# Word conversions five to each of the first three batches, the last one at the beginning of the fourth

## The chip, the cores and the metric

The kernel runs on one core of one Trainium2 chip. The metric is the device time of one execution in microseconds (us). Engines: PE is TensorE, DVE is VectorE, ACT is ScalarE, POOL is GpSimd, and SP is SyncE, which issues all the kernel's DMAs from one queue.

## The reference, cut to what matters

Three layers follow one another: attention over a small memory, a mixture of eight experts that picks one expert per token, and a gated feed-forward layer.

```python
def reference(**kwargs):
    ...
    attn_out = _attn_ref(**attn_kwargs)
    B, H, S, D = attn_out.shape                      # 4, 8, 576, 64
    x = np.ascontiguousarray(attn_out.transpose(0, 2, 1, 3)).reshape(B, S, H * D)
    x = _moe_ref(x=x, **moe_kwargs)
    return _moe2_ref(x=x, **moe2_kwargs)

def _moe2_ref(x, w_in, conv_w, w_out):
    B, S, D_ff = (*x.shape[:2], w_in.shape[1])       # 4, 576, 1024
    K = conv_w.shape[0]                              # 3
    h = np.maximum(x @ w_in, 0.0)
    ...                                              # conv_out: three taps of conv_w along the tokens
    gate = 1.0 / (1.0 + np.exp(-conv_out))
    return (h * gate @ w_out).astype(np.float32)
```

The two weights of the last layer, `w_in` (512 x 1024) and `w_out` (1024 x 512), arrive as 64-bit floats. The kernel reads them as pairs of 32-bit words and turns them into 32-bit floats on the chip. This is the "word conversion".

## The kernel before, in words

**Two phases.** In the first phase the four batches b = 0 to 3 go through attention and through the expert of the batch's first token. In the second phase (`gated`, L801) the four batches go through the last layer: per batch eight blocks f of hidden columns (`pi`, PSUM from `banks`, two buffers, L159), each followed on ACT and DVE by the chain `ht` (L839), `ct` (L841), the two convolution steps (L842, L844), the sigmoid (L820), the product (L821) and the split into `g` (L825, by the helper lines L170 on ACT and L171 on DVE or POOL). Then the output product `po` (L860) runs over all `g` of the batch.

**The written order.** `order()` (L62) writes out the order of the first phase. Each batch has 24 places i: places 0 to 7 are `h` (six matmuls each, `ph`), 8 to 11 are `y` (24 matmuls each, `py`), then again eight `h` and four `y`. After each place the list `after[i]` names further work. PE follows this list exactly (`manual_schedule`, L722). For the other engines and for the DMA queue the order is fixed when the kernel is built, by a planner that goes by the program's order, by what depends on what, and by an estimate of the times. It is not decided anew while the kernel runs: each engine works through its list in order.

**A word conversion.** There are 16, numbered 0 to 15: 0 to 7 make `w_in`, 8 to 15 make `w_out`. Number i has a load of 512 KB into a `words` tile (two buffers, L273, L274), then two ACT steps (L234 takes the size of the high words, L240 scales the low words) and seven DVE steps (L235 to L239, L241, L242), which use two tiles `nd` and `nt` of the tag `nar` (two buffers in all, L281, L282), and a store of 256 KB to `f_in` or `f_out` in DRAM (L284). So number i+1 can't write its `nt` before number i has read its own for the last time (L241), nor its `nd` before the store of i has landed. The load of i+2 can only start when i has read its words for the last time (L242). L234 is held behind what the program put on ACT before it (`keep_in_program_order`); nothing holds L240 back but its load. `narrow_next()` (L75) puts conversion i at a place and, behind it, the load of i+2. The first two loads stand after place 0 of batch 0.

**Who needs them.** `wi0` to `wi3` are loaded from `f_in`, `wo0` to `wo3` from `f_out`, `wo3` from conversions 14 and 15.

**Memory between the phases.** The tiles `vw`, `h`, `words`, `nar` and `ys` of the first phase lie in one pool (`ffn`, L621). It is closed at L892, and the pool of `g`, `tail` and `ot` opens behind it (L893) on memory that it left, each tile waiting for the tiles that it covers (`reuse_waits="tile"`). `ht` and `ct` share six buffers of the tag `cv` (L838, L840, pool at L696). A `ct` is held until its `g` has been split.

Of the kernel before, what the change touches and what calls it, by code (L numbers as in the profile page):

```python
# [57 lines left out]
def units(b):  # L58
    return 2 * b, 2 * b + 1


def order():  # L62

    held = [0]

    def each(c, *parts):
        return [f"{part}.{u}" for u in units(c) for part in parts] if c < B else []  # L70

    def of(c, *parts):
        return [f"{part}.{c}" for part in parts] if c < B else []

    def narrow_next():  # L75

        i = held.pop(0) if held else 16
        return ([f"nar.{i}"] if i < 16 else []) + [f"nload.{i + 2}"] * (i < 14) + (held.append(i + 1) or [])

    out = ["phi.0", "phi.1", "gates", "kv.0", "kv.1", "phi.2", "phi.3", "q.0", "q.1", "kv.2", "kv.3"]  # L80
    out += each(0, "psoft") + each(0, "pback") + each(1, "psoft") + ["mem.0", "mem.1", "back.0", "back.1", "gatew.0", "gatew.1", "frow.0"]
    out += ["fcol.0", "flog.0", "pback.2", "scores.0.0", "scores.1.0", "ssoft.0.0", "ssoft.1.0"]
    out += ["asplit.0.0", "asplit.1.0", "pback.3", "scores.0.1", "scores.1.1", "ssoft.0.1", "ssoft.1.1"]
    out += each(1, "mem") + each(1, "back") + ["asplit.0.1", "asplit.1.1", "vw.0.0", "q.2", "q.3", "gatew.2", "gatew.3", "vw.0.1"]
    for b in range(B):
        c, d = b + 1, b + 2
        u, v = units(c)
        whole = c < B
        after = {i: [] for i in range(24)}
        for i, more in {  # L90
            1: of(c, "frow"),
            3: [f"scores.{u}", f"ssoft.{u}"] * whole,
            8: of(c, "fcol") + [f"scores.{v}", f"ssoft.{v}"] * whole,
            9: of(c, "flog"),
            10: each(d, "pback"),
            11: each(d, "mem")[:1],
            12: each(c, "asplit"),
            13: each(d, "mem")[1:],
            16: each(d, "back"),
            18: each(d, "gatew"),  # L100
            19: of(c, "rtok"),
            21: of(c, "vw0"),
            22: of(c, "vw1"),
        }.items():
            after[i] += more

        if d < B:
            after[2] += each(d, "phi", "kv")
            after[8] += each(d, "psoft")
            after[14] += each(d, "q")  # L110
        if b == 0:
            after[0] += ["w2.0.0", "w2.0.1", "nload.0", "nload.1"]
            after[2] += ["w2.0.2", "w2.0.3"]
            after[9] += ["rtok.0"]
        else:
            after[1] += [f"w2.{b}.3"]
        if whole:
            for i, j in ((21, 0), (22, 1), (23, 2)):
                after[i] += [f"w2.{c}.{j}"]
            for i in (5, 9, 13, 17):  # L120
                after[i] += narrow_next()
            if b == 1:
                after[18] += ["conv"]
        else:
            after[0] += ["rall"]
            after[5] += ["rpp"]
            after[8] += ["rown"]
            after[9] += ["close"]
            for i in (10, 12, 14, 16):
                after[i] += narrow_next()  # L130
            for kc, i in enumerate((12, 14, 17, 20)):
                after[i] += [f"win.{kc}"]
        for i in range(24):
            out += [f"h.{b}" if i % 12 < 8 else f"y.{b}"] + after[i]
    return out
# [6 lines left out]
def fused_kernel(tc, q, first, kv, kv_tail, phi, w1, w2, w_in, conv_w, w_out, out):  # L142
# [3 lines left out]
    with (  # L146
# [565 lines left out]
        def stage_expert(b, g):  # L712
# [6 lines left out]
            "win": lambda kc: stage_w1(lambda: src_in, kc, f"wi{kc}"),  # L719
        }  # L720
        plan = order()
        with tc.manual_schedule(engines={ENG.PE}):  # L722
            for table in (loads, do):
# [228 lines left out]
```

## Time and profile before

| what | value |
|---|---|
| time, median of 3 runs | 456.09 us (455.87 to 458.81) |
| the profiled execution, its own time | 460.18 us |
| its span, first to last instruction | 458.4 us |
| PE busy / DVE busy / ACT busy / POOL busy | 429.5 / 304.2 / 226.1 / 42.2 us |
| mean granted TensorE clock | 0.987 of full speed |

The profiled execution took 1.8 us more than its span, and is 4.1 us longer than the median of the three runs. A busy time counts an engine from the start to the end of its instructions. The ends of matmuls are modelled, so the progress of PE is read better from the number of matmuls in a stretch than from its busy share. "Idle before" an instruction is the time for which its engine stood still, with what ended that.

### The profile page before, as it was taken

What the parts mean: (1) busy time and instruction counts of PE and PEld (TensorE: products, weight loads), DVE (VectorE), ACT (ScalarE), POOL (GpSimd) and SP (SyncE); (2) the same over time, 40 slices, a digit from 0 to 9 for tenths busy, and PEclk for the clock granted to TensorE, in tenths of its full rate; (3) what the DMA queues carried; (4) which work ended last, traced back from release to release, by engine and by line L of the source; (5) the groups of instructions that cost most, each with busy time, mean ns of one, the idle gap of its engine ahead of it and who ended that gap; (6) DMA issues with size and microseconds to landing.
All of it is one profiled execution on the core that took longest, in us unless ns stands there. A gap on an engine that the chain in (4) does not pass through costs nothing.

```text
span 458.4 us, 7910 instructions
## 1 busy us (share of the span) xinstructions
PE 429.5 (94%) x3082; PEld 382.5 (83%) x3083; DVE 304.2 (66%) x566; ACT 226.1 (49%) x432; POOL 42.2 (9%) x64
## 2 busy tenths in 40 slices
PE   3588999998999899999999959999999999999994
PEld 2345898887988689979999958899988998899884
DVE  2379974679956698796899789637920688058700
ACT  4347455454453534456736547247731675157511
POOL 1000000000000000000000006201420043003400
PEclk9999989899999999999999989999999999999999
DMA  7999979443695406988554311320002000100011
GB/s 250 345 346 375 352 284 371 134 159 126 198 358 156 154 15 193 388 292 297 130 190 153 129 49 43 104 92 1 1 35 79 3 2 0 70 23 1 1 71 51
DMA packets 28750, 69.02 MB, mean 151 GB/s; under 512 B 3200, under 2 KB 8576, under 8 KB 28704
## 3 DMA queue, kind: packets, MB, share of 16 engines
q1 hardware_dynamic: 28704, 68.43, 43.9%
q8 instruction: 26, 0.43, 0.4%
q14 instruction: 20, 0.16, 0.1%
HBM read 51.82 MB, written 16.59 MB: 149 GB/s over the span
## 4 chain that ended last, share of the span: by engine, by line
PE 82%; DVE 5%; DMA 5%; ACT 2%; issue 2%; SPq 1%; ACTq 0%
PE po L860 21%; PE py L181 21%; PE pi L181 19%; PE ph L181 10%; PE pv L632 3%; DMA kv<-in_kv 2%; PE pl L514 2%; PE pk L383 2%; PE sc L407 2%; DMA wo2r<-f_out 1%; DMA n4r<-in_w_in 1%; DMA n9r<-in_w_out 1%; DVE wb L171 1%; PE pa L369 1%; PE pfb L486 1%
## 5 line engine op out<-in xcount | busy, mean ns | idle before, releaser
L181 PEld LDWEIGHTS py<-h,wb 128*128 128x128 f32 x768 | 105.9, 194 | 6.3 <-issue 2.9
L181 PE MATMUL py<-h,wb 128*128 128x288 f32 x768 | 110.9, 302 | 0.0
L181 PE MATMUL pi<-yh,wi 128*128 128x288 f32 x512 | 92.1, 298 | 4.8 <-ACT ht L839 4.8
L860 PE MATMUL po<-wo,g 128*128 128x512 f32 (+1 forms) x408 | 89.8, 377 | 0.0
L860 PEld LDWEIGHTS po<-wo,g 128*128 128x128 f32 x408 | 73.0, 188 | 13.4
L181 PEld LDWEIGHTS pi<-yh,wi 128*128 128x128 f32 x512 | 77.3, 191 | 6.0 <-ACT ht L839 5.3
L842 DVE SCALAR_TENSOR_TENSOR ct<-ht,convw,ct 128x575 f32<-128x575 f32 x32 | 30.4, 950 | 51.6 <-ACT ct L841 51.6
L181 PE MATMUL ph<-att,vh 128*128 128x288 f32 x256 | 53.8, 303 | 3.4 <-DVE h L646 3.4
L826 POOL CAST tail<-g 128x128 fp32r<-128x128 f32 x32 | 22.4, 706 | 373.9 <-DVE g L171 373.3
L181 PE MATMUL pi<-yl,wi 128*128 128x288 f32 x256 | 55.2, 297 | 0.0
L181 PEld LDWEIGHTS ph<-att,vh 128*128 128x128 f32 x256 | 40.5, 188 | 7.6 <-DVE h L646 5.2
L181 PEld LDWEIGHTS pi<-yl,wi 128*128 128x128 f32 x256 | 41.6, 191 | 0.0
L839 ACT ACTIVATE ht<-pi 128x576 f32<-128x576 f32 x32 | 20.8, 651 | 36.6 <-PE pi L181 35.7
L645 ACT ACTIVATE h<-ph 128x288 fp32r<-128x288 f32 x64 | 25.4, 410 | 25.6 <-PE ph L181 25.5
L181 PE MATMUL ph<-att,vl 128*128 128x288 f32 x128 | 37.6, 294 | 0.0
L646 DVE SCALAR_TENSOR_TENSOR h<-ph,h 128x288 fp32r<-128x288 f32 x64 | 27.4, 444 | 10.4 <-ACT h L645 10.4
L821 DVE TENSOR_TENSOR ct<-ht,ct 128x576 f32<-128x576 f32 x32 | 27.9, 871 | 6.7 <-ACT ct L820 6.5
L884 ACT ACTIVATE ot<-po 128x512 f32<-128x512 f32 x17 | 9.5, 598 | 41.6 <-PE po L860 41.6
L690 ACT ACTIVATE ys<-py 128x288 f32<-128x288 f32 x32 | 13.0, 407 | 31.7 <-PE py L181 16.6
L170 ACT ACTIVATE g<-ct 128x576 fp32r<-128x576 f32 x32 | 21.3, 679 | 13.8 <-DVE ct L821 13.8
L844 DVE SCALAR_TENSOR_TENSOR ct<-ht,convw,ct 128x575 f32<-128x575 f32 x32 | 26.0, 811 | 0.2
L841 ACT ACTIVATE ct<-ht,convw 128x576 f32<-128x576 f32 x32 | 24.6, 769 | 1.3 <-DVE ct L821 1.0
(246 smaller groups left out, 546.2 us busy)
## 6 DMA issues: line engine op xcount, KB each, us to landing
kv<-in_kv SPq DMA_DIRECT2D x8, 1024.0 KB, 12.2
q<-in_q SPq DMA_DIRECT2D x8, 576.0 KB, 8.7
ydram<-ys SPq DMA_DIRECT2D x32, 144.0 KB, 2.3
y<-ydram SPq DMA_DIRECT2D x4, 1152.0 KB, 5.6
out<-ot SPq DMA_DIRECT2D x15, 256.0 KB, 2.2
ph<-in_phi SPq DMA_DIRECT2D x8, 288.0 KB, 9.9
adram<-at SPq DMA_DIRECT2D x8, 288.0 KB, 6.4
wa_0r<-in_w SPq DMA_DIRECT2D x4, 512.0 KB, 4.1
```

Source lines behind the costliest of these rows:

```text
L170: nc.scalar.activation(hi, src, AF.Copy)
L181: nc.tensor.matmul(ps, st, mv[:, cols], start=i == 0, stop=i == len(terms) - 1)
L632: nc.tensor.matmul(ps[slot_rows(pr)], vs[:, slot_rows(pr)], raws[pr][:, cols], start=True, stop=True)
L645: nc.scalar.activation(t[:, 0, :], ps, AF.Relu)
L646: nc.vector.scalar_tensor_tensor(t[:, 1, :], ps, 0.0, t[:, 0, :].bitcast(F32), ALU.max, ALU.subtract)
L821: slow(f"gm.{f}").tensor_tensor(ct, ht, ct, ALU.mult)
L826: nc.gpsimd.tensor_copy(tail[:, f, :, to:to + 64], t[:, :, 512:576].bitcast(F32))
L839: nc.scalar.activation(two(ht), halves(ps), AF.Relu)
L841: nc.scalar.activation(ct, ht, AF.Copy, scale=convw[:, 1, f:f + 1])
L842: nc.vector.scalar_tensor_tensor(ct[:, 1:], ht[:, :S - 1], convw[:, 0, f:f + 1], ct[:, 1:], ALU.mult, ALU.add)
L844: nc.vector.scalar_tensor_tensor(ct[:, :S - 1], ht[:, 1:], convw[:, 2, f:f + 1], ct[:, :S - 1], ALU.mult, ALU.add)
L860: nc.tensor.matmul(ps[:, cols], st[sp], w[:, mp, f % 2, cols], start=f == 0 and i == 0, stop=f == 7 and i == 2)
```

## The change

Conversions stand after other places. In batches 0 to 2 there are five each, after places 4, 7, 10, 13 and 16, where there were four after places 5, 9, 13 and 17. So these batches hold conversions 0 to 14 instead of 0 to 11. In batch 3, number 15 stands after place 1, where numbers 12 to 15 stood after places 10, 12, 14 and 16. The call after place 3 of batch 3 comes to number 16, which doesn't exist, and adds nothing. Each conversion takes its store and the load of the next but one along. No instruction is added or removed.

```diff
         if whole:
             for i, j in ((21, 0), (22, 1), (23, 2)):
                 after[i] += [f"w2.{c}.{j}"]
-            for i in (5, 9, 13, 17):
+            for i in (4, 7, 10, 13, 16):
                 after[i] += narrow_next()
             if b == 1:
                 after[18] += ["conv"]
         else:
...
             after[5] += ["rpp"]
             after[8] += ["rown"]
             after[9] += ["close"]
-            for i in (10, 12, 14, 16):
+            for i in (1, 3):
                 after[i] += narrow_next()
             for kc, i in enumerate((12, 14, 17, 20)):
                 after[i] += [f"win.{kc}"]
```

## Rows read from the trace of the kernel before

**Rows 1.** The page, part 1: busy time, share of the span, instructions.

```profile
PE 429.5 (94%) x3082; PEld 382.5 (83%) x3083; DVE 304.2 (66%) x566; ACT 226.1 (49%) x432; POOL 42.2 (9%) x64
```

**Rows 2.** Stretches: length, busy us (count) of PE, PEld, DVE, ACT, POOL; clock; DMA; GB/s.

```profile
42.00:99.90 57.90, 57.19 (x473) 50.62 (x471) 44.09 (x91) 29.98 (x66) 0.00 (x0) 0.94 0.80 274
99.90:155.50 55.60, 54.14 (x463) 47.10 (x462) 43.56 (x93) 27.16 (x61) 0.00 (x0) 1.00 0.60 203
155.50:205.00 49.50, 48.15 (x356) 42.73 (x356) 40.51 (x92) 22.83 (x47) 0.00 (x0) 1.00 0.58 202
252.60:277.60 25.00, 20.21 (x142) 19.74 (x141) 19.53 (x30) 14.63 (x23) 3.13 (x4) 0.93 0.31 101
277.60:300.00 22.40, 22.40 (x103) 18.63 (x102) 16.56 (x20) 10.47 (x18) 7.68 (x8) 1.00 0.23 80
```

**Rows 3.** Chain that ended last, in order of time: start, us, what.

```profile
96.79 4.21 DMA n4r<-in_w_in
...
299.63 12.77 PE pi L181 x96
```

**Rows 4.** Timeline between the phases: start, us, engine, line, operation [idle before].

```profile
248.24 0.75 DVE L821 TENSOR_TENSOR ct<-ht,ct 128x576 f32<-128x576 f32 x1
...
270.53 0.69 DVE L242 TENSOR_TENSOR nd<-nd,n15r 128x512 f32<-128x512 f32 x1
...
272.28 0.65 ACT L839 ACTIVATE ht<-pi 128x576 f32<-128x576 f32 x1 [0.88 <-DVE ct L821]
272.83 2.96 ACT L170 ACTIVATE g<-ct 128x576 fp32r<-128x576 f32 x5
...
272.99 0.85 PE L181 MATMUL pi<-yh,wi 128*128 128x288 f32 x2 [4.02 <-ACT ht L839]
```

**Rows 5.** Stretches of 2 us behind that idle time, columns as in rows 2.

```profile
270.00:272.00 2.00, 0.00 (x0) 0.00 (x0) 1.79 (x3) 0.68 (x1) 0.00 (x0) 1.00 0.00 0
...
274.00:276.00 2.00, 2.00 (x10) 2.00 (x9) 1.73 (x3) 2.00 (x5) 1.53 (x3) 0.50 0.78 182
```

**Rows 6.** L234, first step of seven conversions: ns min/median/max, first and last start.

```profile
L234 ACT ACTIVATE nt<-n0r x1: 672/672/672, 58.8 to 58.8; 128x512 f32<-128x512 f32 x1
...
L234 ACT ACTIVATE nt<-n3r x1: 681/681/681, 96.3 to 96.3; 128x512 f32<-128x512 f32 x1
...
L234 ACT ACTIVATE nt<-n7r x1: 690/690/690, 141.8 to 141.8; 128x512 f32<-128x512 f32 x1
...
L234 ACT ACTIVATE nt<-n8r x1: 663/663/663, 164.8 to 164.8; 128x512 f32<-128x512 f32 x1
...
L234 ACT ACTIVATE nt<-n11r x1: 681/681/681, 197.6 to 197.6; 128x512 f32<-128x512 f32 x1
...
L234 ACT ACTIVATE nt<-n12r x1: 670/670/670, 225.4 to 225.4; 128x512 f32<-128x512 f32 x1
...
L234 ACT ACTIVATE nt<-n15r x1: 664/664/664, 262.6 to 262.6; 128x512 f32<-128x512 f32 x1
```

**Rows 7.** Groups by line and shape: busy us, mean ns of one, idle before.

```profile
L237 DVE SCALAR_TENSOR_TENSOR nd<-nt,nd 128x512 int32<-128x512 int32 x16 | 10.9, 682 | 0.2
...
L236 DVE TENSOR_SCALAR nd<-nt 128x512 int32<-128x512 int32 x16 | 6.7, 419 | 6.7 <-DMA f_out<-nd 4.4 <-DMA f_in<-nd 2.3
```

**Rows 8.** Timeline at the starts of batches 1 and 2, and before batch 2.

```profile
101.08 0.68 ACT L240 ACTIVATE n4r<-n4r 128x512 f32<-128x512 uint32 x1 [3.08 <-DVE nd L238]
...
104.68 0.53 PE L181 MATMUL ph<-att,vh 128*128 128x288 f32 x2 [1.31 <-DVE h L646]
...
147.14 0.67 ACT L240 ACTIVATE n8r<-n8r 128x512 f32<-128x512 uint32 x1 [3.38 <-DMA n8r<-in_w_out]
...
156.88 0.67 ACT L240 ACTIVATE n9r<-n9r 128x512 f32<-128x512 uint32 x1 [3.56 <-DMA n9r<-in_w_out]
...
160.47 0.54 PE L181 MATMUL ph<-att,vh 128*128 128x288 f32 x2 [1.35 <-DVE h L646]
```

**Rows 9.** The load of conversion 7: us from its issue to its landing.

```profile
DMA to landing us min/median/max: 9.8/9.8/9.8
```

## The prediction

> **What bounds the kernel now.** I read the page first: PE is busy for 94% of the span [rows 1], so the bound is PE, and only time in which PE stands or runs slowly can be won. The chain that ended last says the same. So I went through stretches of the span for places where PE does fewer matmuls than it could. The last layer gives the full pace: 96 `pi` matmuls in 12.77 us, 0.133 us each [rows 3]. From 300 us on, PE never falls behind it before the last stores. The large loss lies between the phases. From 252.60 to 277.60 PE does 142 matmuls in 25.00 us [rows 2], nearly all of them `pi`; at full pace they take 142 x 0.133 = 18.9 us. So 6.1 us are lost there. The timeline shows how: PE stands for 4.02 us until 272.99, because ACT drains the PSUM buffer (`ht`, L839) only at 272.28 [rows 4], and behind this idle time PE runs at a granted clock of 0.50, ten matmuls in 2 us [rows 5].
>
> Why is ACT late? `ht` waits for a `cv` buffer, which DVE frees with L821. Two things hold DVE and these buffers up, and both are conversions. First, DVE still does conversions: the last ends at 270.53 + 0.69 = 271.22 [rows 4]. Second, the split into `g`, which frees `ct`, comes very late: the first product was ready at 248.24 + 0.75 = 248.99, yet its split starts only at 272.83, and five splits follow one another at once [rows 4]. By the code `g` lies on memory that the pool of the conversions leaves, and behind the last `y` (about 252.6) the conversions are the only work left in that pool. So I read the five splits as released by the end of conversion 15, or as put behind it by the planner, which sees the same dependence. With three `ct` held, six buffers don't suffice, and PE stops.
>
> **The change part by part.** Nothing is added or removed, so the whole price lies in where the conversions now end and in what they disturb on the way.
>
> *The end of the conversions.* They are a chain: `nar` and `words` have two buffers each, so a conversion starts about when its predecessor ends. Starts of L234 [rows 6]: from number 0 to 3, (96.3 - 58.8)/3 = 12.5 us each; from 8 to 11, (197.6 - 164.8)/3 = 10.9; from 12 to 15, (262.6 - 225.4)/3 = 12.4. From 7 to 8 it takes 164.8 - 141.8 = 23.0, from 11 to 12 it takes 225.4 - 197.6 = 27.8: these two wait for their place in the next batch. Under the change places stand three apart and these two waits go. Number 0 starts no earlier than now, I assume: its load is issued behind other loads, and the place moves by one `h` only. Then number 15 starts at 58.8 + 15 x 11.7 = 234 (222 at 10.9 each, 246 at 12.5) and ends 271.22 - 262.6 = 8.6 us later: 243, at worst 255. So the chain ends before PE has only `pi` left, or just behind it, instead of 18.6 us behind.
>
> *What this gives.* A conversion costs DVE three steps like L236 and four like L237 (the other two-source steps taken at its price): 3 x 0.419 + 4 x 0.682 = 4.0 us [rows 7]. Numbers 14 and 15 and the last two steps of 13 lie behind 252: 2 x 4.0 + 2 x 0.68 = 9.4 us of DVE's 19.53 in the stretch [rows 2]. Is DVE then fast enough? From 252.6 to 300.0 it is busy 19.53 + 16.56 = 36.1 us [rows 2]; without 9.4 that is 26.7 in 47.4 - 6.1 = 41.3 us. So it has cover, and `g` can be split from about 255 on. I take all of 6.1 us as gain. Bounds: 0 if the chain ends as late as now, 6.1 at most, as PE is then at full pace. If one conversion still runs behind 252.6, DVE has 30.7 in 41.3 us and still covers it.
>
> The half clock is 6.1 - 4.02 = 2.1 us of this at most, with a short stop before it. The row shows clock 0.50 behind the idle time [rows 5]. The Trainium skill, page "TensorE: Matmul & The Clock Gate", section "What's actually happening", says that the gate goes by a free-running window, so that the number of slow matmuls differs between runs. By that, a run in which the slow stretch is missing anyway would gain only 4.0 us and end at 456.1 - 4.0 + 0.7 = 452.8, inside the forecast's own range below; the sum doesn't use this.
>
> *What the moved conversions cost in batches 0 to 2.* Three more conversions lie there: 12 us of DVE, and 3 x 2 x 0.67 = 4 us of ACT. DVE is busy 44.09 of 57.90, 43.56 of 55.60 and 40.51 of 49.50 us [rows 2]; with 4.0 more each it is at 83, 86 and 90%. So the work fits, but its place matters, because ACT and DVE work in order. At two batch starts this shows: L240 stands at ACT's head waiting for its load (number 4 for 3.08 us, number 9 for 3.56), behind it wait `ys`, the last `wb` and `h`, and PE stands for 1.31 and 1.35 us. Number 8 waits 3.38 us in the midst of `py`, and PE loses nothing [rows 8]. So 12 conversions now cost PE 2.7 us, 0.22 each. Three more at that rate: 0.7 us. Bounds: -2.7 if none meets a batch start any more, and +4.0 if each of the three meets one at 1.35.
>
> On SP's queue a store waits at the head until its L242 is done, and loads of `wa`, `wb` and `ys` stores stand behind it. Three more pairs of store and load move ahead of those of batches 1 to 3. DMA shares there are 0.80, 0.60 and 0.58 [rows 2], so I cost this at nothing; its price if a weight comes late is that of the second rival. Loads of `wo2` and `wo3` come earlier, off PE's path.
>
> *Sum.* -6.1 + 0.7 = -5.4 us. The profiled execution of 460.18 us becomes 454.8. The median of the runs is 4.1 us below that execution; I take the same difference there: 456.09 - 5.4 = 450.7 us.
>
> **The rivals.** *The chain stays late.* If five conversions in a batch slow one another (DVE at 90% in batch 2, ACT held at its head, stores landing late), the pace goes from 11.7 to 13.5 us, and number 15 ends at 58.8 + 15 x 13.5 + 8.6 = 270, as now. Then nothing is won: 456.1 + 0.7 = 456.8, "no change". For it: DVE is nearly full around 160 to 200. Against it: number 12 began 27.8 us behind 11, and this wait surely goes; two of the three paces seen include batches with DVE as busy.
>
> *ACT held at its head, slower than before.* The planner expects loads earlier than they land (3.08, 3.38 and 3.56 us of waiting [rows 8]). The load of number 7 took 9.8 us [rows 9]. Were such a load to meet a batch start, L240 would wait some 9.8 - 4.2 = 5.6 us longer than that of number 4, whose load took 4.21 us [rows 3], and PE would stand 1.3 + 5.6 = 6.9 us, every us above about 1.8 going straight to PE (3.08 - 1.31). One such start eats the gain: 450.7 + 5.6 = 456.3. At two it is 461.9, slower than before. For it: five conversions a batch make it likelier that one is at its load when the batch changes, and the whole order on ACT, DVE and SP is dealt anew. Against it: of the waits on loads seen so far none made PE stand for over 1.35 us. The same page of the Trainium skill, section "Architectural detail: the array is 16× 32×32, not 1× 128×128", says that the queues of ScalarE and VectorE are strictly first in, first out; the rows agree, as `ys` and `wb` stood behind L240.
>
> *The batch starts come free as well.* If none of the conversions meets one, the 2.7 us go too: 456.1 - 6.1 - 2.7 = 447.3.
>
> **How the numbers follow.** A difference under 1% (4.6 us) is about what a measurement of this kernel can't tell from no change. Chances: the forecast 0.50 (450.7; its own range 449 to 453), batch starts free 0.12 (447.3), chain late or one long stop 0.25 (456 to 457), ACT held twice or more, or another order that costs as much, 0.13 (461.9). Predicted is the likeliest, 450.7. The range takes in the free batch starts and the late chain: 447.0 to 457.0; outside stays about 0.15. Faster by over 1% means below 451.5: the free starts and some three quarters of the forecast, 0.12 + 0.37 = 0.49. Slower means above 460.6: 0.12. Within: 0.39.
>
> **What would show it.** Right: L234 of number 15 starts near 234 and no conversion step runs behind 255; the first split of `g` comes within a few us of the last `y`; `pi` of batch 0 runs without idle time and without a clock of 0.50 between the phases; `po` starts some 6 us earlier relative to the last `y`. Batches 0 to 2 have their matmuls in 57.9, 55.6 and 49.5 us, give or take 1.4. Wrong: conversions behind 260, or splits of `g` that still come late though the conversions are over (then another wait held them), or idle times of PE above 1.4 us at batch starts with L240, L234 or a late `wa` or `wb` before them.

## The result and the profile after

| kernel | median | single runs |
|---|---|---|
| before | 457.45 us | 455.87 to 461.06 (4 runs) |
| changed | 452.67 us | 450.98 to 454.13 (4 runs) |

The ratio is 0.9878, with a 95% interval of 0.9841 to 0.9915. Run once more beside other kernels (below), the changed kernel came to 0.985 (0.9813 to 0.9888). So the change makes the kernel faster by 1.2 to 1.5%; the two intervals together reach from 0.9 to 1.9%. 450.7 us was forecast, a gain of 5.4 us. The ratio stands for a gain of 5.6 us; the measured median lies 2.0 us above the forecast.

The profiled executions took 460.18 us and 454.13 us, 6.05 us apart. The timeline of PE shows where they part. The first lines of batch 3, before and then changed (start, us, engine, line, operation):

```profile
206.10 0.43 PE L181 MATMUL ph<-att,vh 128*128 128x288 f32 x2
```

```profile
206.30 0.42 PE L181 MATMUL ph<-att,vh 128*128 128x288 f32 x2
```

Up to there the changed kernel is 0.2 us behind. From there to the end of the span it takes 452.3 - 206.3 = 246.0 us, where the kernel before took 458.4 - 206.1 = 252.3. All of the gain lies behind the start of batch 3.

The stretches of the changed kernel, by the starts of its batches (columns as in [rows 2]): batches 0 to 3, then the `pi` matmuls behind the last `y`.

```profile
40.30:99.20 58.90, 58.10 (x488) 51.07 (x487) 46.55 (x98) 31.90 (x68) 0.00 (x0) 0.97 0.84 287
99.20:157.20 58.00, 55.95 (x464) 48.98 (x463) 45.30 (x98) 28.73 (x64) 0.00 (x0) 0.97 0.58 195
157.20:206.30 49.10, 48.96 (x362) 43.51 (x362) 43.96 (x99) 23.69 (x48) 0.00 (x0) 1.00 0.67 242
206.30:257.00 50.70, 50.64 (x381) 49.67 (x380) 44.56 (x80) 30.17 (x52) 0.00 (x0) 1.00 0.51 174
257.00:273.00 16.00, 16.00 (x119) 15.81 (x119) 13.21 (x17) 11.99 (x19) 5.55 (x6) 1.00 0.20 59
```

The last row answers to the fourth of [rows 2]: 119 matmuls in 16.00 us, 0.134 each, the full pace of [rows 3], with PE busy throughout. The stretches of [rows 2] don't begin with the batches. In the kernel before, the first `h` of batches 0 to 3 begin at 40.04, 100.10, 155.86 and 206.10, so its batches take 60.1, 55.8 and 50.2 us, where the rows here have 58.9, 58.0 and 49.1. Batch 1 is longer; part of it is clock, 0.97 instead of 1.00.

The timeline of the changed kernel between the phases (answers to [rows 4]):

```profile
255.10 0.76 DVE L821 TENSOR_TENSOR ct<-ht,ct 128x576 f32<-128x576 f32 x1
255.77 0.70 DVE L241 TENSOR_TENSOR n15r<-n15r,nt 128x512 f32<-128x512 f32 x1
...
257.51 0.69 DVE L242 TENSOR_TENSOR nd<-nd,n15r 128x512 f32<-128x512 f32 x1
...
259.28 0.65 ACT L839 ACTIVATE ht<-pi 128x576 f32<-128x576 f32 x1 [1.66 <-PE pi L181]
259.97 0.78 ACT L841 ACTIVATE ct<-ht,convw 128x576 f32<-128x576 f32 x1
260.65 1.82 ACT L170 ACTIVATE g<-ct 128x576 fp32r<-128x576 f32 x3
```

Conversion 15 ends at 257.51 + 0.69 = 258.20, not at 271.22, and the first splits of `g` come at 260.65, not at 272.83. `ht` (L839) now waits for PE, where it made PE wait before. The 2.45 us between the end of the conversion and the first split are not a wait for memory alone: ACT has `ht` and `ct` of the next block ahead of the split in its list.

Four stretches of 2 us in the same place (the second and the fourth answer to [rows 5]): the clock stays at 1.00 and PE does 17, 17, 13 and 11 matmuls. The last two stretches have the broader matmuls of `po`.

```profile
268.00:270.00 2.00, 2.00 (x17) 2.00 (x17) 1.97 (x3) 0.92 (x2) 1.09 (x2) 1.00 0.00 0
270.00:272.00 2.00, 2.00 (x17) 2.00 (x17) 1.85 (x3) 1.70 (x4) 0.00 (x0) 1.00 0.00 0
272.00:274.00 2.00, 2.00 (x13) 1.80 (x13) 1.97 (x3) 2.00 (x5) 1.27 (x1) 1.00 0.00 0
274.00:276.00 2.00, 2.00 (x11) 1.65 (x10) 2.00 (x3) 2.00 (x5) 1.26 (x3) 1.00 0.00 0
```

First steps of conversions in the changed kernel (answers to [rows 6]):

```profile
L234 ACT ACTIVATE nt<-n3r x1: 672/672/672, 95.5 to 95.5; 128x512 f32<-128x512 f32 x1
...
L234 ACT ACTIVATE nt<-n8r x1: 675/675/675, 148.3 to 148.3; 128x512 f32<-128x512 f32 x1
...
L234 ACT ACTIVATE nt<-n12r x1: 679/679/679, 191.3 to 191.3; 128x512 f32<-128x512 f32 x1
...
L234 ACT ACTIVATE nt<-n15r x1: 654/654/654, 236.8 to 236.8; 128x512 f32<-128x512 f32 x1
```

The two long waits of the chain are gone: from number 7 (141.0) to 8 it is 7.3 us instead of 23.0, from 11 (179.8) to 12 it is 11.5 instead of 27.8.

### The profile page after: what moved, and what is told of

Same layout as the page of the kernel before. It is cut to its first block, busy times and chain, and to the rows that moved or that the text cites. A ratio compares the mean times of both kernels' runs of the same rounds, so it can differ in the third digit from the quotient of the medians.

```text
span 452.3 us, 7899 instructions
## 1 busy us (share of the span) xinstructions
PE 428.4 (95%) x3082; PEld 381.7 (84%) x3083; DVE 302.6 (67%) x566; ACT 226.7 (50%) x432; POOL 42.6 (9%) x64
## 4 chain that ended last, share of the span: by engine, by line
PE 80%; DMA 8%; DVE 7%; issue 2%; ACT 2%; SPq 1%; ACTq 0%
PE pi L181 22%; PE po L860 22%; PE py L181 20%; PE ph L181 8%; DMA f_in<-nd 3%; DMA kv<-in_kv 3%; PE pv L632 2%; PE pl L514 1%; DMA n6r<-in_w_in 1%; PE sc L407 1%; PE pk L383 1%; DMA n4r<-in_w_in 1%; DVE wb L171 1%; DVE h L646 1%; DVE nd L242 1%
## 5 line engine op out<-in xcount | busy, mean ns | idle before, releaser
L181 PE MATMUL pi<-yh,wi 128*128 128x288 f32 x512 | 90.5, 295 | 0.0
L842 DVE SCALAR_TENSOR_TENSOR ct<-ht,convw,ct 128x575 f32<-128x575 f32 x32 | 29.8, 933 | 54.8 <-ACT ct L841 54.8
L839 ACT ACTIVATE ht<-pi 128x576 f32<-128x576 f32 x32 | 20.8, 651 | 35.4 <-PE pi L181 35.3
L821 DVE TENSOR_TENSOR ct<-ht,ct 128x576 f32<-128x576 f32 x32 | 27.6, 862 | 7.2 <-ACT ct L820 7.1
L844 DVE SCALAR_TENSOR_TENSOR ct<-ht,convw,ct 128x575 f32<-128x575 f32 x32 | 28.3, 883 | 0.3
L170 ACT ACTIVATE g<-ct 128x576 fp32r<-128x576 f32 x32 | 21.4, 679 | 13.2 <-DVE ct L821 13.2
```

The source lines that it names most:

```text
L170: nc.scalar.activation(hi, src, AF.Copy)
L181: nc.tensor.matmul(ps, st, mv[:, cols], start=i == 0, stop=i == len(terms) - 1)
L821: slow(f"gm.{f}").tensor_tensor(ct, ht, ct, ALU.mult)
L839: nc.scalar.activation(two(ht), halves(ps), AF.Relu)
L842: nc.vector.scalar_tensor_tensor(ct[:, 1:], ht[:, :S - 1], convw[:, 0, f:f + 1], ct[:, 1:], ALU.mult, ALU.add)
L844: nc.vector.scalar_tensor_tensor(ct[:, :S - 1], ht[:, 1:], convw[:, 2, f:f + 1], ct[:, :S - 1], ALU.mult, ALU.add)
```

## The experiments

Three theories were set against one another. **M**: `g` lies on the memory of the conversions, `ct` stays held until the last conversion is done, the six `cv` buffers run out, and PE stops. **D**: DVE is late because it still has conversion steps to do, wherever their tiles lie. **R**: the gain comes from the new deal of the lists in batches 0 to 2.

### Conversions in memory of their own

Room had to be made for this, so the control has the same smaller buffers.

```diff
-            p = lp.tile([128, S], F32, tag="p", bufs=2, name=f"p{name}")
+            p = lp.tile([128, S], F32, tag="p", bufs=1, name=f"p{name}")
...                                      # both ot tiles:
-                            ot = gp.tile([128, 256], F32, tag="ot", bufs=4, ...
+                            ot = gp.tile([128, 256], F32, tag="ot", bufs=2, ...
```

> Control for the two kernels beside it: the order of before, with two `ot` buffers instead of four and one `p` buffer instead of two, which makes room in SBUF. Theory M (memory): same as before within 2 us, since the conversions still lie in the pool that `g` takes over; the first split of `g` behind the end of conversion 15, near 272, and PE idle for about 4 us before it. Theory D (DVE's load) and theory R (a new deal of the lists): the same.

456.44 us, ratio 0.996 (0.9935 to 0.9986): 0.4% faster by itself, within what was expected. In the profiled execution PE waits for `ht` for 3.4 us in two stops, and the first split of `g` comes at 267.19, right behind the end of conversion 15 (266.46 + 0.68 = 267.14).

```diff
-                words[i] = fps[0].tile([128, 1024], I32, tag="words", bufs=2, name=f"n{i}r")
+                words[i] = wpool.tile([128, 1024], I32, tag="words", bufs=2, name=f"n{i}r")
...
-            d = fps[0].tile([128, 512], F32, tag="nar", bufs=2, name=f"nd{i}")
-            t = fps[0].tile([128, 512], I32, tag="nar", bufs=2, name=f"nt{i}")
+            d = wpool.tile([128, 512], F32, tag="nar", bufs=2, name=f"nd{i}")
+            t = wpool.tile([128, 512], I32, tag="nar", bufs=2, name=f"nt{i}")
```

> The order of before (four conversions a batch, the last four in batch 3), but `words` and `nar` lie in the pool that stays open, so no `g` covers them; two `ot` buffers and one `p` buffer make the room. Theory M (`g` waits for the memory of the conversions, `ct` stays held, PE stops): the first splits of `g` come near 257, long before conversion 15 ends; the idle time of PE of 4 us between the phases and the slow clock behind it go; time 4 to 6 us below before, ratio about 0.988. Theory D (the stop comes from the 9.4 us of conversion steps on DVE behind 252, wherever the tiles lie): the stop stays at 3 us or more, ratio 0.995 to 1.003. Theory R (the gain came from the new deal of the lists in batches 0 to 2): ratio 1.0.

452.81 us, ratio 0.9888 (0.9861 to 0.9915), as M expected, 3.6 us below its control. The timeline of ACT in this kernel:

```profile
257.24 0.40 ACT L690 ACTIVATE ys<-py 128x288 f32<-128x288 f32 x1
258.94 0.65 ACT L839 ACTIVATE ht<-pi 128x576 f32<-128x576 f32 x1 [1.31 <-PE pi L181]
259.49 1.25 ACT L170 ACTIVATE g<-ct 128x576 fp32r<-128x576 f32 x2
...
269.77 0.67 ACT L234 ACTIVATE nt<-n15r 128x512 f32<-128x512 f32 x1
```

Two `g` are split 2 us behind the last `ys`, ten microseconds before conversion 15 even begins. Between the phases PE no longer waits for `ht` at all; one wait of 1.2 us remains, of `po` for the split of a late `wo`. DVE does the same conversion steps here as in the kernel before, later still. So D falls: the steps on DVE alone don't stop PE. R falls as well, since batches 0 to 2 keep the old order.

> The changed order (five a batch, the last in batch 3 after place 1) with the same own memory for `words` and `nar`. Theory M: the change has already taken the stop away, so nothing more is won: time of the changed kernel, ratio to before about 0.988, difference to e1_own_memory under 2 us. Theory D: as M here. Theory R: as the changed kernel.

The changed order with both edits: 453.88 us, ratio 0.9901 (0.9876 to 0.9925), 1.1 us from the one above, intervals overlapping. The two remedies don't add up: they take away the same stop. With memory of their own and the changed order, the first split comes 2.5 us behind the start of the last `ys` (260.24 and 257.75), in the changed kernel 3.4 us behind it (260.65 and 257.21), so the shared memory hardly holds `g` back any more there.

### More `cv` buffers

```diff
-            late.append(tc.tile_pool(name="late", bufs=6, side="right", reuse_waits="tile"))
+            late.append(tc.tile_pool(name="late", bufs=8, side="right", reuse_waits="tile"))
```

> The kernel before with eight `cv` buffers instead of six; nothing else. Theory M says that the stop comes about because `ct` stays held while `g` has no memory, and six buffers run out at the sixth block. With eight, one more block gets its `ht` and `ct` before the buffers run out: the first split of `g` still comes behind the end of conversion 15 (270 to 273), but the idle time of PE before it falls from 4.8 us to under 2; ratio to before 0.988 to 0.995. If the stop came from DVE being late with its steps whatever the buffers, the idle time stays at 4 us or more and the ratio at 0.998 to 1.002.

453.77 us, ratio 0.9905 (0.9869 to 0.9941). The order of before, so conversion 15 is still late and `g` with it, but PE's wait for `ht` is gone. From the timeline:

```profile
273.89 0.68 DVE L242 TENSOR_TENSOR nd<-nd,n15r 128x512 f32<-128x512 f32 x1
...
274.65 2.96 ACT L170 ACTIVATE g<-ct 128x576 fp32r<-128x576 f32 x5
```

The splits start 0.08 us behind the end of conversion 15 (273.89 + 0.68 = 274.57), which shows the first link of M almost bare. Whether ACT waits there for the memory itself, or its list has the splits at that place because of the memory, the trace doesn't tell. That two buffers more take the stop away shows the second link, the six `cv` buffers. What is left is 2.0 us of waiting for `yh` and `yl` of batch 1, whose matmuls now come early.

### The last four conversions early, alone

```diff
-            for i in (10, 12, 14, 16):
+            for i in (1, 3, 5, 7):
                 after[i] += narrow_next()
```

> One part alone: batches 0 to 2 keep four conversions after places 5, 9, 13 and 17, and only the last four move, to places 1, 3, 5 and 7 of batch 3. With a pace of 11.7 us number 12 starts near 208, number 15 near 243 and ends near 254 to 260. Theories M and D: nearly the whole gain, 4 to 6 us below before, ratio 0.987 to 0.991, no idle time of PE above 1 us between the phases. Theory R (batches 0 to 2 gave the gain): ratio 0.997 to 1.003.

453.98 us, ratio 0.9922 (0.9898 to 0.9946): 3.6 us by the ratio, most of the gain, a little under what was expected. The chain goes 205.8, 216.9, 235.5, 255.3 for numbers 12 to 15, so number 15 is 12 us later than forecast and ends at 265.31. The splits start at 267.58, and between the phases PE has one wait of 0.8 us for a `g`, none for `ht`. With batches 0 to 2 as before, R falls a second time.

### One conversion late

```diff
-            for i in (1, 3):
+            for i in (23,):
                 after[i] += narrow_next()
```

> The change, but conversion 15 stands after the last place (23) of batch 3 instead of place 1; 0 to 14 stand as in the change. So only one conversion (4 us of DVE) lies behind the last `y`, but the pool stays held to its end, near 264 to 266. Theory M (`g` waits for the memory of the last conversion): the first split of `g` comes within 3 us behind that end, so between the changed kernel (260.65) and the one before (272.83); six `cv` buffers still suffice for about all of that, so PE stands for 0 to 2 us; ratio to before 0.988 to 0.994. Theory D (DVE's load): with 4 us instead of 9.4 the stop is gone and the splits come right behind the last `y`; ratio 0.988.

452.87 us, ratio 0.9857 (0.9778 to 0.9935). From the timeline:

```profile
261.92 0.69 DVE L242 TENSOR_TENSOR nd<-nd,n15r 128x512 f32<-128x512 f32 x1
...
264.30 2.40 ACT L170 ACTIVATE g<-ct 128x576 fp32r<-128x576 f32 x4
```

One late conversion holds the splits back until 264.30 (last `ys` at 255.89), which only M says. But PE doesn't stop: up to there six buffers suffice. The stop has a threshold. Counted from the end of the last `y` matmul, the conversions end 6.8 us later here and 9.5 us later in the run above (265.31), both without a wait of PE for `ht`; in the kernel before they end 18.3 us later, with 4.8 us of idle time. Between 9.5 and 18.3 us the six buffers run out.

### The last four later still

```diff
-            for i in (10, 12, 14, 16):
+            for i in (14, 17, 20, 23):
                 after[i] += narrow_next()
```

> The order of before, with the last four conversions still later: after places 14, 17, 20 and 23 of batch 3 instead of 10, 12, 14 and 16. Number 12 then starts some 6 us later than the 225.4 of before, number 15 near 269, and it ends near 277. Theory M: the first split of `g` moves with it, to 277 to 280, and the stop of PE grows by as much, 5 to 7 us; ratio 1.010 to 1.016. Theory D: the same 9.4 us of steps, or 3 us more of them, lie behind 252; the stop grows by at most 3 us; ratio 1.000 to 1.007.

457.2 us, ratio 0.9978 (0.9941 to 1.0016). M's numbers missed, and D's lowest, 1.000, lies inside the interval; but the edit hardly moved what it was to move, so this says nothing between M and D. Number 12 starts at 229.1 (3.7 us later), but number 15 at 262.1, and it ends at 270.75. The stop is the one of before, 4.7 us. The places don't set the end. Numbers 13 and 14 start at 235.2 and 252.9, 0.2 and 0.4 us behind the last use of `nt` by their predecessors (L241, ending at 234.98 and 252.51), as the two buffers demand, and how long a conversion takes hangs on what else stands in DVE's list.

### Six in a batch

```diff
-            for i in (4, 7, 10, 13, 16):
+            for i in (3, 6, 9, 12, 15, 18):
                 after[i] += narrow_next()
...
-            for i in (1, 3):
+            for i in ():
```

> Six places a batch in batches 0 to 2 (3, 6, 9, 12, 15, 18), so that all 16 conversions stand ahead of batch 3. If the chain through the two `nar` buffers sets the end (starts 11.7 us apart), number 15 ends where it does in the changed kernel, 258 give or take 4, and the time is that of the changed kernel: ratio 0.985 to 0.991. If the places set the end, number 15 starts near 190 and ends before 215, and the splits of `g` come right behind the last `y`; the time is the same, as PE has no stop to lose. If conversions in batches 0 to 2 cost PE 0.22 us each or more, it is slower than the changed kernel by 0.2 us for one (not to be told apart) or by more for a new stop at a batch start.

453.33 us, ratio 0.9858 (0.9778 to 0.9937). Number 15 starts at 236.6, where it starts in the changed kernel (236.8), though its place is now the one after place 12 of batch 2, with seven `h` and four `y` still to come before batch 3. The chain sets the end. One conversion more in batches 0 to 2 costs nothing that can be told apart.

### The stop at the start of a batch

Two runs were about the 1.0 us of idle time that is left at the start of batch 1.

```diff
-            nc.scalar.activation(lowf, low.bitcast(U32), AF.Copy, scale=2.0 ** -52)
+            first(nc.scalar.activation(lowf, low.bitcast(U32), AF.Copy, scale=2.0 ** -52))
```

> The change, and L240 (the second ACT step, the one that stood at ACT's head waiting for its load) is held behind L234 of its conversion by the same call that holds L234. Theory A (L240 at ACT's head makes PE stand at the start of batch 1): the waits of ACT for loads of words go, and with them the idle time of 1.0 us of PE at that start; time 1 to 2 us below the changed kernel, ratio 0.983 to 0.988. Rival (the last `wb` of a batch comes late by its own load or by DVE): the idle time at the start of batch 1 stays at 0.8 us or more; ratio 0.987 to 0.991.

453.57 us, ratio 0.9929 (0.9899 to 0.9959), no faster than the changed kernel. ACT's waits for loads at L240 are gone, but the stop stays, 0.94 us, and one of 1.18 us stands at the start of batch 2, which the changed kernel doesn't have. The timeline of DVE and PE there:

```profile
99.74 1.22 DVE L171 TENSOR_TENSOR wb<-wb_3r,wb 128x1024 fp32r<-128x1024 f32 x1
100.87 0.68 DVE L241 TENSOR_TENSOR n3r<-n3r,nt 128x512 f32<-128x512 f32 x1
101.47 0.45 DVE L646 SCALAR_TENSOR_TENSOR h<-ph,h 128x288 fp32r<-128x288 f32 x1
...
101.98 0.53 PE L181 MATMUL ph<-att,vh 128*128 128x288 f32 x2 [0.94 <-DVE h L646]
```

ACT had done its part of the first `h` by about 100; DVE does the split of `wb` and a conversion step first. So with the wait of L240 gone, DVE's own list makes PE stand for as long.

```diff
-ON_POOL = {"gs.3", "gs.4", "gs.6"}
+ON_POOL = {"gs.3", "gs.4", "gs.6", "w2.1.3", "w2.2.3", "w2.3.3"}
```

> The change, with the second half of the split of the last `wb` piece of batches 1 to 3 (L171, 1.22 us on DVE at the start of each batch) on POOL, which does nothing in that phase. Theory V (at the batch starts PE waits for `h` on DVE because that split stands before it in DVE's list): the idle time of PE at the start of batch 1 falls from 1.0 us to under 0.3, that at batches 2 and 3 likewise; time 0.5 to 2 us below the changed kernel run beside it. Rival (another step of the list stands there, or ACT is late): the idle time stays at 0.8 us or more, time within 0.5 us.

456.29 us, ratio 0.9977 (0.995 to 1.0005), 4.9 us above the changed kernel beside it; neither expectation holds. The split left DVE, but what stood behind it grew longer:

```profile
100.01 2.37 POOL L171 TENSOR_TENSOR wb<-wb_3r,wb 128x1024 fp32r<-128x1024 f32 x1 [97.70 <-ACT wb L170]
...
100.58 2.35 DVE L241 TENSOR_TENSOR n3r<-n3r,nt 128x512 f32<-128x512 f32 x1
```

PE still waits for `h` for 2.3 us in four stops; at the start of batch 1 it is 0.32 and then 0.79 us, where the changed kernel has one of 1.01. The profiled execution was the fastest of the ten (453.11 us, clock 0.992), so this trace doesn't show the slower ones. Part of the 4.9 us is clock: the mean granted clock of eight of its ten runs is 0.984 to 0.988, and 0.993 in three of the four runs beside it (450.5 to 452.0 us, 1.1 to 2.6 us below that profiled execution). Why the clock is lower there was not settled. What would take the small stops at batch starts away stays open; the rows point to the order of DVE's list.

> The changed kernel itself once more, beside the other two on the same chip: ratio to before 0.984 to 0.992 by either theory; PE has no idle time of `pi` between the phases; conversion 15 starts at 234 to 240.

451.4 us, ratio 0.985 (0.9813 to 0.9888), number 15 done at 259.10, no idle time of PE between the phases. No version was faster than the changed kernel.

## Why the prediction was right, and where it wasn't

*The bound and the place.* Right. PE was the bound, and the gain came from behind the start of batch 3: 6.3 us in the profiled pair for 6.1 forecast. 4.8 us of it are the two waits for `ht`; the remaining 1.5 us fit the stretch at a granted clock of 0.50 that followed [rows 5] and that the changed kernel doesn't have. This part isn't there in every run: the profiled execution of the control with smaller buffers has the stop (3.4 us) and a granted clock of 1.00 from 200 to 300 us.

*The cause.* Half right. The prediction named two things, the memory under `g` and 9.4 us of conversion steps on DVE. The runs show that the stop needs the first and that the second doesn't make it by itself: with the steps later still and only the memory apart, PE's wait for `ht` went. Whether the memory alone, without DVE's steps, would have stopped PE for as long, no run shows. In the kernel before, six of them stand between 265.7 and 271.2 among the steps that free `cv` buffers.

*The end of the conversions.* The start was right and the end wrong. Number 15 starts at 236.8 (forecast 234, range 222 to 246). But it takes 258.20 - 236.8 = 21.4 us instead of the 8.6 taken from the row of number 15 before, so it ends at 258.2, behind the "worst" of 255. The failed step is that term. DVE was full while number 15 ran before (busy for 8.55 of the 8.62 us), but with few other steps between its own. Number 13, which ran almost wholly ahead of the last `y`, took 18.7 us there (235.1 to 253.8) and would have been the nearer row. In the changed kernel number 15 runs ahead of the last `y` too, and DVE does its steps between those of the next phase, without a pause, as this stretch shows:

```profile
240.00:250.00 10.00, 10.00 (x78) 10.00 (x77) 10.00 (x19) 6.19 (x9) 0.00 (x0) 1.00 0.49 164
```

It cost nothing, because of the threshold that the runs show: conversions that end up to 9.5 us behind the last `y` leave PE no wait for `ht`, and these end 1.1 us behind it. The prediction didn't work out this threshold, and its "255" was not derived from it. That the gain held although the end came 15 us behind the forecast was luck, as far as the prediction goes.

*The cost in batches 0 to 2.* Forecast +0.7 us. From the first `h` of batch 0 to that of batch 3 it is 166.1 us before and 165.9 us in the changed kernel (40.36 to 206.30), at a mean granted clock of 0.98 in both: no cost that can be told apart. Batch 1 took 2.2 us more, beyond the 1.4 that the prediction allowed, with a granted clock of 0.50 from 140 to 142 us; the other two took less. PE's waits fell from 3.6 to 2.9 us. Those of the changed kernel from 40 to 205 us (engine, line, waited for: total, times, longest), where [rows 8] has stops of 1.31 and 1.35:

```profile
PE ph L181 <- DVE h L646: 1.6, 2, 1.0
PE pfb L486 <- DVE fw L477: 0.6, 1, 0.6
PE ph L181 <- DVE vl L171: 0.3, 1, 0.3
PE ph L181 <- ACT vwg L418: 0.2, 1, 0.2
PE py L181 <- DVE h L646: 0.2, 1, 0.2
```

*The price by L240.* Half right as a mechanism, and not a price per conversion. For the kernel before, the trace bears the reading of [rows 8] out. Between L240 (101.08) and PE's start (104.68) stand these:

```profile
101.95 1.05 ACT L170 ACTIVATE wb<-wb_3r 128x1024 fp32r<-128x1024 f32 x1
...
103.03 1.23 DVE L171 TENSOR_TENSOR wb<-wb_3r,wb 128x1024 fp32r<-128x1024 f32 x1 [1.55 <-ACT wb L170]
...
104.18 0.45 DVE L646 SCALAR_TENSOR_TENSOR h<-ph,h 128x288 fp32r<-128x288 f32 x1
```

DVE stands idle until ACT, late by L240, has written `wb`, and PE waits for the `h` behind it. But holding L240 back took those waits away and left the stop, with DVE's list as the next limit. And the 0.22 us a conversion doesn't hold: with 15 conversions in place of 12, one such stop is left (1.01 us) instead of two.

*The rivals.* The late chain did not come: the waits for places went as forecast, though the length of the last conversion shows that DVE can slow the chain. The long wait of ACT at a batch start did not come either; number 7's load again took 9.7 us, in the middle of a batch. The batch starts didn't come free as well: one stop of 1.01 us is left.

*The difference between profile and median.* Taken as 4.1 us on both sides, it was 2.7 us before, by the median of four runs, and 1.5 us after. Single runs of one kernel lie up to 7 us apart, so this term of the sum is uncertain by more than the forecast's error of 2.0 us.

## What to carry to other kernels

When a pool opens on memory that another pool leaves, ask which work is last to use that memory: one slow side job can hold back the first tiles of the next phase, though the engine that does it has time. Look for the row where several like instructions start at once behind something unrelated, and test it by giving the side job its own memory or the waiting tiles more buffers. And where a chain runs through two buffers, its pace sets its end; moving its places further ahead does nothing once it no longer waits for them.

## What the runs showed of the hardware that was not expected

In the run with the `wb` split on POOL, a DVE step and a POOL step that stood side by side did not share: the conversion step L241 took 2.35 us while POOL's split ran from 100.01 to 102.38, where it takes 0.68 us otherwise. The Trainium skill, page "SBUF — State Buffer", section "SBUF: two separate sides", speaks of a port pair that DVE with two SBUF inputs and GpSimd hold exclusively for a whole instruction, so that the other waits; this run agrees, since DVE's step, with both inputs in SBUF, ended 0.55 us behind POOL's. In the changed kernel L844 (1.89 us instead of 0.82) and one L821 (1.32 instead of 0.75) likewise end 0.6 us behind a POOL split of `g`.

TensorE also fell to half its clock without standing still before. In the kernel before, two stretches inside batch 0 have a granted clock of 0.50, the lower of its two levels (1.2 GHz), with PE busy throughout:

```profile
62.00:64.00 2.00, 2.00 (x10) 2.00 (x10) 2.00 (x9) 0.00 (x0) 0.00 (x0) 0.50 0.15 54
...
82.00:84.00 2.00, 2.00 (x10) 2.00 (x10) 1.90 (x4) 0.90 (x3) 0.00 (x0) 0.50 0.03 8
```

Both follow the 24 matmuls of `pl` with nine columns each (57.98 to 60.19 and 79.62 to 81.78). Not every `pl` is followed by one: in the changed kernel the second and the third of the four `pl` are followed by such a stretch, and in the control with smaller buffers none is. In the profiled execution of that control PE ran at a mean granted clock of 0.999 (452.79 us, the fastest of its ten runs), in that of the kernel with own memory at 0.984 (458.43 us, the slowest of five), and its other four runs at 0.994 to 0.998. So the mean granted clock varies between runs of one kernel, and the time with it. Where the clock fell in the runs without a trace is not known.
